# Another order for the first five visits of a fused retention and feed-forward kernel, and two chunks turned on another engine

## The chip, the cores and the metric

The kernel runs on one core of one Trainium2 chip. The metric is the device time of one execution in microseconds (us). A NeuronCore has five engines that run their own instruction streams side by side and wait for each other through semaphores: TensorE (PE: matmuls and transposes; PEld is its loading of stationary operands), VectorE (DVE), ScalarE (ACT), GpSimd (POOL) and SyncE (SP, whose queue here issues nearly all DMA transfers). Each stream is executed strictly in the order in which it was written, so the order of the program text is the schedule.

## The reference

```python
def _attn_ref(q, k, v):              # (8, 8, 576, 64) float32
    scores = (1 / sqrt(64)) * q @ k^T
    gamma = 1.0 - 2.0 ** (-5.0 - arange(8))          # one per head
    Dmat = where(rel >= 0, gamma ** rel, 0.0)        # rel = i - j
    return (scores * Dmat) @ v
def _moe_ref(x, w_in, w_out):        # x: the above as (4608, 512)
    h = maximum(x @ w_in, 0.0)       # w_in (512, 2048)
    return (h * h) @ w_out           # w_out (2048, 512)
```

So: a causal retention over 8 batches and 8 heads, whose output is laid out as 4608 tokens by 512 features, and a feed-forward layer with a squared ReLU. `w_in` and `w_out` arrive as 64-bit floats and the rest as 32-bit floats; the computation is in 32-bit floats.

## The kernel before

**Chunks and visits.** Each batch's 576 tokens are cut into four chunks of 128 and one of 64: 40 chunks in all (chunks 4, 9, 14, ... are the short ones). The main loop (L740 to L812) makes one *visit* per chunk. Visit i first works on the retention of chunk i-1 in three pieces, `retain_a`, `retain_b`, `retain_c` (64x64 matmuls at L457, L460 and L492; ScalarE copies the state at L466 and L495, and the finished, transposed output `xT` at L514), and computes the scores of chunk i (L435), which VectorE multiplies by the causal mask (L441 for chunks 0 to 3, L443 later). GpSimd multiplies q and v by the decay factors (`scale_q`, L375, and L445).

**Turning.** The scores need q and k with the head dimension on the partitions. This is done in two ways. `turn(i)` (L406) makes 16 TensorE transposes (8 for a short chunk, L414); ScalarE copies the k half out (L417) and VectorE the q half (L418). The other way is `flip(i)` (L388), two VectorE transposes of 32x32 blocks (L392), followed by `spread(i)` (L394), which queues 16 small ScalarE copies (8 for a short chunk, L403) that `move` issues a few at a time. `N_TURN, N_BACK = 9, 19` (L380) say that chunks 9 to 18 go the second way; chunk i is flipped in visit i-2 and spread at the end of visit i-1. With `turn`, the same PSUM tile `ps_t` holds the transposes and, from chunk 4 on, the scores.

**Block 0 of the feed-forward layer.** Tokens are taken in 9 blocks of 512. Block 0 is done plainly: 16 *pieces* of `w_in` (128 of the 2048 columns each), each converted on the chip from 64-bit to 32-bit floats and then used in `first_in(j)` (L570): four matmuls of 512 columns (L580), a ReLU on ScalarE (L585), and a square on VectorE that is queued and issued later (L588). `first_in(j, (0,))` and `first_in(j, (1,))` do one half of the tokens each, with 256 columns; the first half of block 0 is there after chunk 1, the second only after chunk 3. `N_HALF = 4` pieces are done in halves.

**Conversions.** A piece is converted in six steps (`round_parts`, L199): one and two on VectorE (L210, L214), *beside*, two ScalarE instructions (L218, L219), and three, four, five on VectorE (L222, L225, L228). `convert(n)` issues the next n steps. From piece 4 on, one and two of the next piece are issued between *beside* and three. After five of a piece, SP fetches up to two later pieces (`fetch_raw`, L196) into six raw buffers.

**The other blocks.** Blocks 1 to 8 are done by Strassen's scheme with seven products (`ffn_in`, 28 steps per block, eight PE records of 256 columns each, L616), with sums on VectorE (L540 to L543 for the inputs, L554 to L557 for the results, L238 to L241 for the weights, during block 1). The first 13 steps of block 1 also convert the first two pieces of `w_out`. A planner, `ffn(i, half)` (L698), is called twice in each visit: while block 0 lasts it issues one first_in and six conversion steps in the first half of a visit and two of each in the second; afterwards it interpolates in the table `PACE` (L691) how many steps should be done by the tokens gone. Blocks become available when their tokens are complete (in `retain_c`): block 1 in visit 9.

**SP's queue.** `load(i+3)` at the end of visit i fetches q, k and v of a chunk; from visit `N_TURN - 1` on, q and k are fetched a visit earlier. The q scaling of chunk i+3 stands at the end of visit i on GpSimd (L811), behind which the v scaling of later chunks queues.

After the visits comes a second phase (from L838, from 595 us on in the trace) that multiplies by `w_out`; the change does not touch it.

Of the kernel before, what the change touches and what calls it, by code (L numbers as in the profile page):

```python
# [40 lines left out]
def kernel(  # L41
# [50 lines left out]
    N_CH = len(chunks)  # L92
# [38 lines left out]
    N_EARLY = TOK // C  # L131
# [25 lines left out]
    pieces = [(0, m, e) for m in range(N_M) for e in range(2)]  # L157
    pieces += [(1, mq + mh * N_MQ, e) for mq in range(N_MQ) for mh in range(2) for e in range(2)]
    N_W1 = N_DF
    N_HALF = 4  # L160
    stage = [W[5].rearrange("p (o s f) -> p o s f", o=4, s=NP),
             W[6][:, 0:3 * NP * 128].rearrange("p (o s f) -> p o s f", o=3, s=NP)]
    N_RAW = 6
# [121 lines left out]
    def fetch_raw(count):  # L285

        for _ in range(count):
            if n_raw[0] < min(N_W1, n_made[0] + N_RAW):
                fetch_w(n_raw[0])
                n_raw[0] += 1  # L290


    def w_in_parts():

        parts = [round_parts(j) for j in range(N_W1)] + [[None] * 2]
        for j in range(N_W1):
            one, two, beside, three, four, five = parts[j]
            if j <= N_HALF:
                yield from (one, two)
            yield beside  # L300
            if j >= N_HALF:
                yield from parts[j + 1][0:2]
            yield three
            yield four

            def last(five=five):
                five()
                n_made[0] += 1
                if n_next[0]:
                    fetch_raw(2)  # L310

            yield last

    w_in_steps = w_in_parts()

    def convert(count):
        for _ in range(count):
            f = next(w_in_steps, None)
            f and f()
# [37 lines left out]
    def rows(half, n=64):  # L357
        return slice(64 * half, 64 * half + n)
# [13 lines left out]
    def scale_q(i, engine):  # L372
        ci, cs = chunks[i][1], chunks[i][3]
        t = loaded[i][0][:cs]
        engine.tensor_tensor(t, t, dv[:cs, :, NCH + ci:NCH + ci + 1].to_broadcast([cs, H, D]), op=ALU.mult)  # L375
# [1 line left out]

    N_TURN, N_BACK = 9, 19  # L380
    moves = []

    def new_qk(i):
        t = work3.tile([128, 2, HP, C], F32, tag="qk", name="qk")
        st[i]["qT"], st[i]["kT"] = t[:, 0, :, :], t[:, 1, :, :]
        return t
# [19 lines left out]
    def turn(i):  # L406

        cs = chunks[i][3]
        n_h = cs // CH
        p = ps_t.tile([128, 2, 512], F32, tag="t", name="t_ps").rearrange("p h (j d t) -> p h j d t", j=2, d=HP)  # L410
        for j in (1, 0):
            for hp in range(HP):
                for h in range(n_h):
                    nc.tensor.transpose(p[:, h, j, hp, :], loaded[i][j][rows(h), 2 * hp:2 * hp + 2, :],  # L414
                                        ident[rows(h), rows(h)])
        to = new_qk(i)[:, :, :, :cs].rearrange("p j d (h t) -> p j d h t", h=n_h)
        nc.scalar.copy(to[:, 1].rearrange("p d h t -> p h d t"), p[:, :n_h, 1, :, :])  # L417
        nc.vector.tensor_copy(to[:, 0].rearrange("p d h t -> p h d t"), p[:, :n_h, 0, :, :])  # L418
# [146 lines left out]
    def some(count=1):  # L565
        for f in queue[:count]:
            f and f()
        del queue[:count]

    def first_in(j, halves=(0, 1)):  # L570

        assert n_made[0] > j
        wi, m, e = pieces[j]
        mp, mm = divmod(m, 2)
        p = ps_f.tile([128, 2, HT], F32, tag="f", name="h_ps")
        w = w_in[mp][:, mm, 2 * e:2 * e + 2, :, :].rearrange("p s c f -> p (s c) f")
        lo, hi = halves[0], halves[-1] + 1
        p = p[:, lo:hi, :]
        for c in range(N_DM):
            nc.tensor.matmul(p.rearrange("p h t -> p (h t)"), lhsT=w[:, c, :], rhs=xT[0][:, c, lo * HT:hi * HT],  # L580
                             start=(c == 0), stop=(c == N_DM - 1))

        t = g_room[mp % 2][:, 3:7:3, mm, :] if e else g_room[mp % 2][:, 0:5:4, mm, :]
        t = t[:, lo:hi, :]
        nc.scalar.activation(t, p, AF.Relu)  # L585

        some(2)
        queue.append(lambda: nc.vector.tensor_tensor(t, t, t, op=ALU.mult))  # L588
        if mm and e and hi == 2:
            queue.append(lambda: [nc.sync.dma_start(  # L590
                g_dram[0, a:b, :, 2 * mp:2 * mp + 2, :].rearrange("s p m t -> p s (m t)"),
                g_room[mp % 2][:, a:b, :, :].rearrange("p s m t -> p s (m t)")) for a, b in QUARTERS])
        if j >= N_W1 - 4:

            sums_w.setdefault(0, sum_w_in(0)).pop(0)()
            if n_next[0] > 1:
                if 1 not in sums_x:
                    sums_x[1] = sum_x(1)
                sums_x[1].pop(0)()
# [73 lines left out]

    def block_steps(n):
        if n == 0:
            seconds = [(0, lambda j: (first_in(j, (1,)), first_in(j + 1, (1,))), j) for j in range(0, N_HALF, 2)]
            return seconds + [(0, first_in, j) for j in range(N_HALF, N_W1)]
        return [(n, ffn_in, n, mp, j) for mp in range(N_MP) for j in range(NP)]

    def step():  # L680
        n, f, *args = steps.pop(0)
        done[0] += 1
        f(*args)

    n_next = [0]

    HALF = C // 2
    N_0 = N_W1 - N_HALF // 2  # L690
    PACE = ((4 * TOK + HALF // 4, N_0 + 2 * N_MP * NP - 2), (5 * TOK - HALF, N_0 + 3 * N_MP * NP - 2),  # L691
            (6 * TOK + HALF // 4, N_0 + 4 * N_MP * NP - 2), (8 * TOK + HALF // 4, N_0 + 6 * N_MP * NP - 2),
            (9 * TOK, N_0 + 7 * N_MP * NP - 2))
    done = [0]
# [32 lines left out]
    def warm(count, wide):  # L727
        t = ps_f.tile([128, 512], F32, tag="f", name="idle_ps")
        for _ in range(count):
            if wide:  # L730
                nc.tensor.matmul(t[:, 0:128], lhsT=idle, rhs=idle, start=True, stop=True)
            else:
                for b in range(2):
                    nc.tensor.matmul(t[rows(b), 0:64], lhsT=idle[rows(0), rows(b)], rhs=idle[rows(0), 0:64], start=True, stop=True,
                                     skip_group_check=True)
# [4 lines left out]
    for i in range(N_CH + 1):  # L740
        if i <= N_EARLY:

            if i == 1:
                convert(2)
            elif i == 2:
                convert(5)
            if i >= 1:
                retain_a(i - 1)
                if i < 3:
                    warm(4, False)  # L750
                else:
                    convert(1)
                    first_in(2 * i - 5, (0,))
                    convert(5)
                retain_b(i - 1)
                if i < 3:
                    warm(4, False)
                retain_c(i - 1)
            convert((0, 1, 1, 0, 1)[i])
            if i == N_EARLY:  # L760
                fetch_raw(2)
                step()
            scores(i)
            if i == 2:
                convert(5)
                first_in(0, (0,))
            elif i == 3:
                convert(1)
                first_in(2, (0,))
                convert(5)  # L770
            elif i == N_EARLY:
                convert(5)
                step()
                convert(6)
            scale_q(i + 1, nc.gpsimd)
            if i < N_EARLY:
                if i < 2:
                    warm(6, False)
                turn(i + 1)
        else:  # L780
            if i == N_EARLY + 1:
                gone[0] = TOK
            retain_a(i - 1)
            if i < N_TURN or N_BACK <= i < N_CH:
                turn(i)
            move(C, i)
            ffn(i - 1, 0)
            retain_b(i - 1)
            if i < N_CH:
                scores(i)  # L790
            retain_c(i - 1)
            if N_TURN <= i + 1 < N_BACK:
                spread(i + 1)
            if N_TURN <= i + 2 < N_BACK:
                flip(i + 2)
            ffn(i - 1, 1)
        if i == 0:
            fetch_raw(2)
        if i < N_TURN - 1:
            load(i + 3)  # L800
        else:
            if i == N_TURN - 1:
                load(i + 3, "qk")
            if i + 4 < N_CH:
                load(i + 4, "qk")
            if i + 3 < N_CH:
                load(i + 3, "v")
        if 0 < i < N_EARLY:
            fetch_raw(1)
        if i > N_EARLY:  # L810
            for j in range(i + 1 + 2 * (i > N_EARLY + 1), min(i + 4, N_CH)):  # L811
                scale_q(j, nc.gpsimd)  # L812
    assert n_next[0] == N_BLK
    first.close()
# [231 lines left out]
```

## Time and profile before

| | us |
|---|---|
| median of 4 runs | 992.36 |
| lowest, highest of them | 991.49, 995.08 |
| the profiled execution | 995.08 |
| its span, first to last instruction | 993.4 |
| PE busy in it | 968.8 |
| DVE busy in it | 767.8 |
| ACT busy in it | 242.4 |
| POOL busy in it | 126.6 |

The profiled execution is the slowest of the four. The span lacks the 1.7 us that lie around the instructions. A PE that counts as busy need not be at its peak: its granted clock is listed beside, and short matmuls follow each other more closely than their durations say. In a line of the timeline the figures are the start, the duration, engine, line and operation, the tiles, the number of instructions merged, and in brackets the idle time in front and what ended it.

With `N_CH` = 40 chunks the visits can be found in the trace by their matmuls: visit 4 begins at 36.3 us, visit 5 at 52.5, visit 6 at 65.3, visit 7 at 78.7, visit 8 at 93.6, visit 9 at 107.2.

### The profile page before, as it was taken

To read this page: it belongs to the slowest core of one execution; us is meant where nothing else is said; L and a number is where in the kernel's file an instruction comes from. 1 tells how busy PE (TensorE), PEld (TensorE's weight loads), DVE (VectorE), ACT (ScalarE), POOL (GpSimd) and SP (SyncE) were. 2 spreads that over 40 slices of the span, in tenths; PEclk is the share of its full clock that TensorE was granted. 3 is DMA by queue.
4 is the path that set the end of the run, shared out by engine and by line. 5 is a ranking of instruction groups with operands and counts; after the bars stand their busy time and mean duration, and the time that the engine had idled before them with its cause. 6 is when DMAs were issued, how large, how long until landed. Compare 5 with 4: busy or idle time off the path is not lost.

```text
span 993.4 us, 24367 instructions
## 1 busy us (share of the span) xinstructions
PE 968.8 (98%) x10388; PEld 864.4 (87%) x10388; DVE 767.8 (77%) x1437; ACT 242.4 (24%) x596; POOL 126.6 (13%) x121
## 2 busy tenths in 40 slices
PE   7899999999999999999999999999999999999998
PEld 6654677888888888888888889999999999999998
DVE  3798798767978888897986777877777677777766
ACT  2544675672222222312221000000000000000000
POOL 3202323122121321212111000000000000000000
PEclk9999999999999999999999999999999999999999
DMA  8873757575587678679358999674673757556351
GB/s 199 240 206 119 195 161 216 156 205 171 180 305 212 197 249 262 217 223 285 112 213 293 404 390 351 233 280 170 233 269 138 272 192 274 190 216 217 123 213 43
DMA packets 185036, 219.20 MB, mean 221 GB/s; under 512 B 118624, under 2 KB 135008, under 8 KB 175968
## 3 DMA queue, kind: packets, MB, share of 16 engines
q1 hardware_dynamic: 182816, 217.13, 66.3%
q8 instruction: 81, 1.33, 0.5%
q10 hardware_dynamic: 2112, 0.52, 0.2%
q14 instruction: 27, 0.22, 0.1%
HBM read 128.23 MB, written 89.39 MB: 219 GB/s over the span
## 4 chain that ended last, share of the span: by engine, by line
PE 87%; DVE 8%; ACT 2%; issue 1%; DMA 1%; SPq 0%; DVEq 0%; ACTq 0%
PE o_b L903 17%; PE h_b L616 15%; PE o_c L903 11%; PE o_a L903 11%; PE h_c L616 10%; PE h_a L616 10%; PE h_ps L580 5%; PE x_ps L457 3%; PE sc_ps L435 2%; PE x_ps L492 2%; PE t_ps L414 1%; DVE w L222 1%; DVE room L623 1%; PE u_ps L460 1%; DVE w L225 1%
## 5 line engine op out<-in xcount | busy, mean ns | idle before, releaser
L616 PE MATMUL h_b<-room,w 128*128 128x256 f32 x736 | 177.1, 383 | 4.5 <-DVE room L635 2.3
L616 PEld LDWEIGHTS h_b<-room,w 128*128 128x128 f32 x736 | 137.2, 190 | 25.5 <-DVE room L635 3.5
L903 PE MATMUL o_b<-w,room 128*128 128x128 f32 x1168 | 144.5, 275 | 0.2 <-DVE room L854 0.2
L903 PEld LDWEIGHTS o_b<-w,room 128*128 128x128 f32 x1168 | 137.2, 192 | 0.5 <-DVE room L854 0.4
L903 PE MATMUL o_c<-w,room 128*128 128x128 f32 x1008 | 123.0, 275 | 0.0
L903 PEld LDWEIGHTS o_c<-w,room 128*128 128x128 f32 x1008 | 117.7, 192 | 0.0
L616 PE MATMUL h_c<-room,w 128*128 128x256 f32 x480 | 114.5, 381 | 0.0
L616 PE MATMUL h_a<-room,w 128*128 128x256 f32 x448 | 107.6, 383 | 0.0
L616 PEld LDWEIGHTS h_c<-room,w 128*128 128x128 f32 x480 | 90.3, 190 | 12.8 <-DVE room L642 0.3
L616 PEld LDWEIGHTS h_a<-room,w 128*128 128x128 f32 x448 | 83.7, 190 | 11.8
L903 PE MATMUL o_a<-w,a 128*128 128x128 f32 x688 | 85.6, 275 | 0.0
L633 POOL TENSOR_TENSOR room<-room 128x512 f32<-128x512 f32 x32 | 36.0, 1125 | 368.5 <-ACT room L632 293.1
L903 PEld LDWEIGHTS o_a<-w,a 128*128 128x128 f32 x688 | 81.2, 192 | 0.1
L917 ACT COPY r<-o_a 128x128 f32<-128x128 f32 x53 | 14.1, 266 | 271.8 <-PE o_a L903 236.0
L623 DVE SCALAR_TENSOR_TENSOR room<-room 128x512 f32<-128x512 f32 x96 | 71.0, 740 | 3.3
L580 PE MATMUL h_ps<-room,w 128*128 128x512 f32 (+1 forms) x160 | 60.2, 526 | 3.5 <-DVE w L228 2.9
L403 ACT COPY qk<-flip 32x256 f32<-32x256 f32 x144 | 57.9, 402 | 2.1
L375 POOL TENSOR_TENSOR q_ld<-q_ld,dv 128x512 f32<-128x512 f32 (+1 forms) x39 | 46.1, 1181 | 83.4 <-DMA q_ld<-in_q_dram 52.0
L457 PEld LDWEIGHTS x_ps<-qk,v_ld 64*64 64x64 f32 x1152 | 40.6, 137 | 15.9 <-issue 10.6
L635 DVE TENSOR_TENSOR room<-h_b,room 128x512 f32<-128x512 f32 x32 | 22.0, 688 | 41.5 <-PE h_b L616 41.5
L457 PE MATMUL x_ps<-qk,v_ld 64*64 64x64 f32 x1152 | 49.9, 227 | 3.2 <-ACT u_sb L495 2.2
L580 PEld LDWEIGHTS h_ps<-room,w 128*128 128x128 f32 x160 | 30.1, 195 | 25.5 <-issue 21.1
(111 smaller groups left out, 1437.3 us busy)
## 6 DMA issues: line engine op xcount, KB each, us to landing
g_dram<-room SPq DMA_DIRECT2D x32, 1792.0 KB, 7.8
a<-g_dram SPq DMA_DIRECT2D x43, 1024.0 KB, 6.9
room<-g_dram SPq DMA_DIRECT2D x20, 1024.0 KB, 5.8
w<-w_dram SPq DMA_DIRECT2D x7, 1792.0 KB, 12.1
out_dram<-room SPq DMA_DIRECT2D x17, 512.0 KB, 3.3
w<-in_moe_w_in_dram SPq DMA_DIRECT2D x16, 512.0 KB, 5.3
w<-in_moe_w_out_dram SPq DMA_DIRECT2D x16, 512.0 KB, 4.1
v_ld<-in_v_dram SPq DMA_DIRECT2D x31, 256.0 KB, 3.9
```

The costliest lines, as they stand in the source:

```text
L375: engine.tensor_tensor(t, t, dv[:cs, :, NCH + ci:NCH + ci + 1].to_broadcast([cs, H, D]), op=ALU.mult)
L403: nc.scalar.copy(*moves.pop(0)[1:])
L435: nc.tensor.matmul(sc[e][rows(h), hp, :], lhsT=kT[rows(e), hp, t], rhs=qT[rows(e), hp, t], start=True, stop=True, skip_group_check=True)
L457: own.append(lambda hp=hp, e=e, b=b: nc.tensor.matmul(x_at(hp, b, h), lhsT=s["vs"][rows(h), 2 * hp + b, :], rhs=s["ret"][rows(h), e, hp, : ...
L492: nc.tensor.matmul(x_at(hp, b, h), lhsT=u[rows(e), hp, :], rhs=s["qT"][rows(e), hp, CH * h:CH * h + CH], start=clears(b, hp // 2), stop=Fa ...
L580: nc.tensor.matmul(p.rearrange("p h t -> p (h t)"), lhsT=w[:, c, :], rhs=xT[0][:, c, lo * HT:hi * HT], start=(c == 0), stop=(c == N_DM - 1))
L616: nc.tensor.matmul(p[:, mm, :], lhsT=w[:, c, :], rhs=xs[n][right][:, c, :], start=(j in OPENS and mm == 0 and c == 0), stop=(j in CLOSES a ...
L623: nc.vector.scalar_tensor_tensor(t, t, 0.0, t, op0=ALU.max, op1=ALU.mult)
L633: nc.gpsimd.tensor_tensor(g["A11"], g["A11"], g["A11"], op=ALU.mult)
L635: nc.vector.tensor_tensor(g["A22"], p, p15, op=ALU.add)
L903: nc.tensor.matmul(p, lhsT=s["lefts"][left][:, m, :], rhs=w_out[j][:, m, WO_SLOT[right], :], start=(i in OPENS and m == 0), stop=(i in CLO ...
L917: nc.scalar.copy(r[:, 0, 0:128], p)
```

## The change

The order of the conversions and first products in visits 3 and 4, with the conversion step reached in brackets:

| | before | after |
|---|---|---|
| visit 3, second half | first_in(2, first half), convert (26), turn(4) | first_in(2, first half), convert (24) |
| visit 4, between retain_a and retain_b | convert (27), first_in(3, first half), convert (32) | turn(4) |
| visit 4, after retain_c | convert (33), second halves of 0 and 1 | second half of 0 |
| visit 4, after the scores | convert (38), second halves of 2 and 3, convert (44) | convert (27), second half of 1, convert (32) |

Three pieces are done in halves instead of four. The step list of block 0 becomes 16 entries (three second halves and 13 whole pieces) instead of 14 (two pairs of second halves and 12 whole pieces), at most three entries per visit as before, so it ends in visit 9 and not in visit 8. `PACE` moves by two with it, so its points name the same steps of blocks 1 to 8. Chunks 9 and 10 are turned by `turn`, in visits 9 and 10, and `flip` and `spread` begin with chunk 11. The early loading of q and k begins at visit 10. Up to visit 7, the q scaling that is issued at the end of a visit is that of chunk i+2, not i+3.

```diff
-    N_HALF = 4
+    N_ALONE = 4
+    N_HALF = 3
...
-            if j <= N_HALF:
+            if j <= N_ALONE:
                 yield from (one, two)
             yield beside
-            if j >= N_HALF:
+            if j >= N_ALONE:
                 yield from parts[j + 1][0:2]
...
-    N_TURN, N_BACK = 9, 19
+    N_TURN, N_BACK = 11, 19
...
-            seconds = [(0, lambda j: (first_in(j, (1,)), first_in(j + 1, (1,))), j) for j in range(0, N_HALF, 2)]
+            seconds = [(0, first_in, j, (1,)) for j in range(N_HALF)]
             return seconds + [(0, first_in, j) for j in range(N_HALF, N_W1)]
...
+    n_scaled = [N_EARLY + 2]
...
-    N_0 = N_W1 - N_HALF // 2
+    N_0 = N_W1
...
                 if i < 3:
                     warm(4, False)
+                elif i == N_EARLY:
+                    turn(i)
                 else:
                     convert(1)
-                    first_in(2 * i - 5, (0,))
+                    first_in(1, (0,))
                     convert(5)
...
-            convert((0, 1, 1, 0, 1)[i])
+            convert((0, 1, 1, 0, 0)[i])
...
                 first_in(2, (0,))
+                convert(3)
+            elif i == N_EARLY:
+                convert(3)
+                step()
                 convert(5)
-            elif i == N_EARLY:
-                convert(5)
-                step()
-                convert(6)
...
-                turn(i + 1)
+                if i + 1 < N_EARLY:
+                    turn(i + 1)
...
-            for j in range(i + 1 + 2 * (i > N_EARLY + 1), min(i + 4, N_CH)):
+            for j in range(n_scaled[0], min(i + (4 if i > N_TURN - 4 else 3), N_CH)):
+                n_scaled[0] += 1
                 scale_q(j, nc.gpsimd)
```

## The prediction

> **What bounds the kernel now.** I read the page first (busy shares, the chain that ended last), then the stretches by visit, then PE's gaps in order of time, then the other engines around each gap.
>
> ```profile
> PE 968.8 (98%) x10388; PEld 864.4 (87%) x10388; DVE 767.8 (77%) x1437; ACT 242.4 (24%) x596; POOL 126.6 (13%) x121
> ...
> PE 87%; DVE 8%; ACT 2%; issue 1%; DMA 1%; SPq 0%; DVEq 0%; ACTq 0%
> ```
>
> TensorE is the bound; what can be won without taking work from it is its idle time and the VectorE share of the chain. Where those lie, by stretches (busy per engine, then granted clock, DMA share, GB/s):
>
> ```profile
> 22.20:25.60 3.40, 3.40 (x100) 3.21 (x100) 0.46 (x2) 1.47 (x4) 2.12 (x2) 0.56 0.24 49
> 39.20:42.70 3.50, 3.50 (x40) 2.52 (x38) 1.73 (x3) 1.57 (x3) 0.78 (x1) 0.57 1.01 278
> 35.70:65.30 29.60, 26.79 (x269) 17.38 (x268) 23.04 (x43) 12.53 (x27) 3.16 (x3) 0.94 0.84 236
> 65.30:107.20 41.90, 40.67 (x492) 21.00 (x491) 35.47 (x57) 21.17 (x44) 8.43 (x8) 1.00 0.55 151
> 107.20:159.00 51.80, 47.02 (x589) 38.75 (x590) 47.70 (x71) 34.95 (x85) 14.08 (x11) 1.00 0.69 198
> 159.00:297.00 138.00, 137.94 (x1669) 117.44 (x1672) 107.35 (x170) 60.30 (x145) 31.91 (x29) 1.00 0.66 201
> ```
>
> From 159 us on PE does not stop (0.06 us idle in 138), and the change leaves those steps as they are. What it can move lies in three stretches: visits 4 and 5 (29.60 - 26.79 = 2.8 us idle, and 3.5 us at a clock of 0.57, which wastes 3.5 x 0.43 = 1.5), visits 6 to 8 (1.2 us idle) and visits 9 to 12 (4.8 us idle). The gaps themselves:
>
> ```profile
> 38.87 2.99 PE L580 MATMUL h_ps<-room,w 128*128 128x256 f32 x8 [1.85 <-DVE w L228]
> 44.58 3.72 PE L580 MATMUL h_ps<-room,w 128*128 128x256 f32 x16 [0.68 <-ACT room L514]
> 52.49 0.46 PE L414 MATMUL t_ps<-w,k_ld 64*128 64x64 f32 x8
> 53.13 3.70 PE L580 MATMUL h_ps<-room,w 128*128 128x512 f32 x8
> 85.47 0.69 PE L435 MATMUL sc_ps<-qk 64*64 64x64 f32 x32 [1.23 <-DVE qk L418]
> 108.38 0.69 PE L492 MATMUL x_ps<-qk,u_sb 64*64 64x64 f32 x32 [0.50 <-ACT u_sb L466]
> 113.27 1.97 PE L616 MATMUL h_b<-room,w 128*128 128x256 f32 x8 [0.98 <-DVE room L541]
> 130.46 0.27 PE L457 MATMUL x_ps<-qk,v_ld 64*64 64x64 f32 x2 [0.97 <-DVE qk L443]
> 157.01 1.99 PE L616 MATMUL h_b<-room,w 128*128 128x256 f32 x8 [1.45 <-DVE room L635]
> ```
>
> **The change, part by part.** *Visits 4 and 5.* Before, first_in(3, first half) stands in front of `retain_b(3)` and waits 1.85 us for step five of piece 3; the clock drops, and these 8 records take 2.99 us where the same ones at 29.08 and 33.79 us take 1.97. After, turn(4) stands there. I replay PE by its rows from 35.7 us, where first_in(2) ends: retain_a(3) 0.6 to 36.3 (its mask is done at 35.8); turn(4), 0.64 from its start to the next group (52.49 to 53.13), to 37.0; retain_b, with the state copy done by then, to 37.5; the 0.28 wait for L495 and retain_c to 38.4; the 0.68 wait for the `xT` copy; second half of piece 0 (1.9) to 41.0; scores(4) to 41.6; second half of piece 1 to 43.5; turn(5) to 44.1; second half of piece 2 to 46.0; retain_b(4) to 46.3. Scores(5) then need VectorE's L418 of turn(5), which stands behind the whole conversion of piece 4. VectorE: five(3) ends at 38.7, L418(4) and a square to 39.5; then the mask of scores(4) makes it wait to 42.2 and is done at 42.8; one and two of piece 4 to 43.5, a square, one and two of piece 5 (its data landed at 44.0) to 44.7; three, four, five of piece 4 (0.72 + 0.72 + 0.61) to 46.8; L418(5) to 47.5. So PE waits about 1.3 us there. Waits of 0.28 + 0.68 + 1.3 and 0.2 of loose ends make 2.4, against 2.8 + 1.5 = 4.3 before: **-1.9**. Bounds: SP issues the fetch of piece 5 at 37.6 in both kernels; landings of `w_in` took 3.8 to 7.9 us, 6.4 here. At 7.9 PE waits 1.5 more; a quicker landing gains nothing, since *beside* of piece 4 ends only at 44.8. The clock: the stretch ahead of the drop held only 0.6 us of matmuls; in the replay it holds 2.4. If it drops all the same, +1.5.
>
> The Trainium skill ("TensorE: Matmul & The Clock Gate", section "HAM oscillation — how this bites in real kernels") gives the rule that PE should have no gaps over about 3.4 us. By it neither kernel would lose clock here, and the 1.5 us would stay saved; the trace, where a gap of 1.85 us was followed by 0.57, speaks against leaning on it.
>
> *What moves behind it.* At the end of visit 4 VectorE has 32 conversion steps behind it instead of 44, two pieces, and PE two pieces less: the lead of three pieces, in program order, is the same in visits 5 to 8. On SP, load(7) stands behind two fetches released by five(4), not four: issued at 52.94 before, near 48 now; load(8) still queues behind fetches for five(7), near 60 instead of 69.9.
>
> *Visits 6 to 8.* The one gap, 1.23 us at 85.47, has its cause here:
>
> ```profile
> 81.19 0.69 DVE L222 SCALAR_TENSOR_TENSOR w<-w,w 128x512 f32<-128x512 uint32 x1
> 81.24 1.56 POOL L375 TENSOR_TENSOR q_ld<-q_ld,dv 64x512 f32<-64x512 f32 x1 [3.24 <-DMA q_ld<-in_q_dram]
> 81.91 1.43 DVE L225 TENSOR_TENSOR w<-w,w 128x512 f32<-128x512 f32 x1
> 82.76 1.50 POOL L445 TENSOR_TENSOR v_ld<-v_ld,dv 128x512 f32<-128x512 f32 x1
> 83.38 1.43 DVE L228 SCALAR_TENSOR_TENSOR w<-w,w 128x512 uint32<-128x512 uint32 x1
> 84.73 0.68 DVE L418 COPY qk<-t_ps 128x512 f32<-128x512 f32 x1
> ```
>
> Beside a GpSimd row a VectorE row of 0.69 takes 1.43. Four GpSimd scalings fall into visit 7, because scale_q(8), issued in visit 5, waited 16.8 us for its data with v of chunk 6 behind it. With scaling one visit later v no longer stands behind a q that has not landed, and about two scalings fall into each visit. Also flip(9) and flip(10) (4 rows, 0.66 to 0.69 each) leave visits 7 and 8. I take **-0.8**; bounds -1.2 (gap gone) and +0.7 (one doubled row in each of three visits on the chain to L418, less the 0.5 us that L418(6) came ahead of its scores).
>
> *Visits 9 to 12.* PE gains two turns: 2 x 0.64 = **+1.3**, on the bound engine, hidden by nothing; 0 if they fall into waits. ScalarE loses 8 + 16 copies of 0.40 (9.6 us) and gains two of 0.37 and 0.59; VectorE loses four flip rows (2.7) and gains L418 of 0.41 and 0.68. The 0.50 at 108.38 was such copies ahead of L466: gone. The 0.98 at 113.27 was flip(11), 1.3 us, ahead of block 1's input sums L540 and L541; now flip(11) falls under first_in(15), and one of the sums too: gone, and so the 0.25 in its wake. What remains (0.97, 0.29, 0.28, 1.45: 3.0) is VectorE, 47.7 of 51.8 us busy, under the 13 steps that also convert `w_out`. After, these steps lie in visits 10 and 11 with two flips instead of three in their way, 1.3 us less: 1.7 remain. **-3.0** in all; bounds -4.8 (no idle left) and 0 (the same waits one visit later: `PACE` now asks for 54 steps in 1008 tokens, not in 1104).
>
> *One half piece less.* Two halves take 3.65 us, a whole one 3.53 in a pair: **-0.1**. What comes after visit 14 has the same steps at the same tokens: 0.
>
> Sum: -1.9 - 0.8 + 1.3 - 3.0 - 0.1 = **-4.5 us**. The profiled execution, 995.08, would become 990.6; it lies 2.7 above the median. From the median 992.36 I predict **987.9**.
>
> **The rivals.** *The clock drops anyway* (15%): -4.5 + 1.5 = -3.0, 989.4. For it: 22.20 to 25.60 ran at 0.56 after a gap of 2.65; against: 2.4 us of matmuls in the stretch, if small ones. *VectorE's crowd only moves* (15%): the waits of visits 9 to 12 return in 10 to 13: -4.5 + 3.0 = -1.5, 990.9. For it: 9.8 of 10 us busy there. *The waits are unaffected overall* (5%): whatever closes opens elsewhere, 992.4. *Slower: VectorE bounds block 1* (15%). Place: visits 10 to 14, where two pieces' worth of PE time has to be caught up. A step costs PE 1.73 and its share of a visit's attention about 0.5, 2.23; VectorE has 1.1 (nine sums of 0.61 and three squares of 0.72 in seven steps), 0.4 of weight sums (4 x 0.68 in seven), 0.4 of `w_out` (two pieces of 2.7 in 13) and 0.5 of mask, flip and two doubled rows (3.4 in a visit of seven): 2.4 in the first 13 steps, 2.0 thereafter. It decides from 2.75 per step over some 20 steps: 0.5 x 20 = 10 us of waits instead of 1.7, +8.3, 996.2. Against it: with the same steps and no `w_out`, VectorE has 107 of 138 us from 159 on.
>
> **How the numbers follow.** Forecast 50%, its own range 985 to 990.5 by the bounds above; rivals as given. About 0.3% (3 us) is what a measurement can tell from no change. Below 989.4: nearly all of the forecast, half of the clock rival, a little of the second: 0.56. Above 995.3: the slower rival and mishaps of the data of piece 5: 0.17. Between: 0.27. The range takes in the first two rivals and part of the slower one: 983.8 to 994.5.
>
> **What the profile after would show.** Right: no L580 gap for L228 in visit 4, the clock at 1.00 around 40 us; a gap of about 1.3 before scores(5) for L418; no gap in visit 7; two L414 groups in visits 9 and 10; block 1's first L616 step with no wait for L541. Wrong: a clock near 0.57 in visit 4 or 5; scores of visits 5 to 8 all waiting for L418; L616 gaps of over 2 us in sum in visits 10 to 13.

## The result and the profile after

The changed kernel takes 989.76 us in the median of 43 runs (988.39 to 993.87), the kernel before 992.64 us (65 runs, 990.82 to 996.77). The ratio is 0.9971, with a 95% interval of 0.9965 to 0.9976: 2.9 us faster, 0.3%. The prediction was 4.5 us faster.

The profiled execution of the changed kernel took 989.67 us, close to its median, with a span of 988.0. The profiled execution before, 995.08, lay 2.4 above its own median, so the two spans differ by 5.4 us, of which about half is not the change. Lines of the changed kernel's page (busy shares; the chain that ended last):

```profile
PE 969.0 (98%) x10404; PEld 863.1 (87%) x10404; DVE 769.3 (78%) x1434; ACT 234.2 (24%) x573; POOL 128.3 (13%) x121
...
PE 90%; DVE 7%; ACT 1%; issue 1%; DMA 0%; SPq 0%; DVEq 0%; ACTq 0%
```

PE's busy time is nearly the same (before: 968.8 us, 98%), and more of the chain is PE (before: 87%): waits went. By stretches, with the borders at the beginning of visit 6 (54.6 us), of visit 9 (96.0) and of the scores of chunk 13 (157); columns: length, busy time of PE, PEld, DVE, ACT and POOL, granted clock, DMA share, GB/s:

```profile
35.00:54.60 19.60, 18.25 (x240) 11.96 (x238) 16.27 (x29) 8.40 (x19) 4.74 (x4) 1.00 1.04 276
54.60:96.00 41.40, 40.79 (x489) 21.09 (x488) 37.20 (x60) 21.32 (x42) 6.28 (x5) 1.00 0.64 179
96.00:157.00 61.00, 58.26 (x701) 45.05 (x703) 55.80 (x81) 33.38 (x80) 16.89 (x13) 1.00 0.64 178
157.00:291.50 134.50, 134.48 (x1611) 114.81 (x1606) 105.07 (x167) 56.80 (x137) 30.82 (x28) 1.00 0.70 207
```

PE is idle for 1.35, 0.61 and 2.74 us in the first three and not at all in the fourth; in the first profile before it was 2.8 us (and a stretch at half clock), 1.2 and 4.8. The gaps that are left, in PE's rows of the timeline:

```profile
37.23 0.27 PE L458 MATMUL x_ps<-qk,v_ld 64*64 64x64 f32 x2 [0.28 <-ACT u_sb L496]
38.60 1.99 PE L581 MATMUL h_ps<-room,w 128*128 128x256 f32 x8 [0.68 <-ACT room L515]
46.47 0.69 PE L436 MATMUL sc_ps<-qk 64*64 64x64 f32 x32 [0.38 <-DVE qk L419]
74.22 0.69 PE L436 MATMUL sc_ps<-qk 64*64 64x64 f32 x32 [0.61 <-DVE qk L419]
135.14 1.99 PE L617 MATMUL h_b<-room,w 128*128 128x256 f32 x8 [0.30 <-DVE room L636]
149.16 1.99 PE L617 MATMUL h_c<-room,w 128*128 128x256 f32 x8 [0.65 <-DVE room L631]
152.81 1.99 PE L617 MATMUL h_b<-room,w 128*128 128x256 f32 x8 [1.66 <-DVE room L636]
```

Line numbers are one higher than before. The gap for step five of piece 3 is gone, as are those behind the small ScalarE copies (0.50) and before block 1's sums (0.98). VectorE's backlog in block 1 shows up one or two visits later, in one long gap of 1.66 us.

**A measure that does without the start.** Both kernels run the same instructions up to the scores of chunk 3, yet these begin anywhere from 30.9 to 33.3 us in the profiles below. From the scores of chunk 18 to the last instruction the three profiles compared next take 765.3, 765.3 and 765.4 us, and all profiles of this case 765.1 to 765.7. So I compare the time from the start of the scores of chunk 3 to the start of those of chunk 18, "the stretch": it holds nearly everything that these kernels do differently, and the start's scatter is left out. It is read from one execution of each kernel. It is 195.57 us in the first profile before, 193.52 in a second one (below) and 190.47 after: 3.05 us less than the second.

### The profile page after: what moved, and what is told of

It is laid out like the page before. It is cut to its first block, busy times and chain, and to the rows that moved or that the text cites. A ratio compares the mean times of both kernels' runs of the same rounds, so it can differ in the third digit from the quotient of the medians.

```text
span 988.0 us, 24367 instructions
## 1 busy us (share of the span) xinstructions
PE 969.0 (98%) x10404; PEld 863.1 (87%) x10404; DVE 769.3 (78%) x1434; ACT 234.2 (24%) x573; POOL 128.3 (13%) x121
## 3 DMA queue, kind: packets, MB, share of 16 engines
q8 instruction: 82, 1.34, 0.6%
## 4 chain that ended last, share of the span: by engine, by line
PE 90%; DVE 7%; ACT 1%; issue 1%; DMA 0%; SPq 0%; DVEq 0%; ACTq 0%
PE o_b L909 17%; PE h_b L617 16%; PE o_c L909 11%; PE o_a L909 11%; PE h_a L617 10%; PE h_c L617 10%; PE h_ps L581 5%; PE x_ps L458 3%; PE sc_ps L436 2%; PE x_ps L493 2%; PE t_ps L415 2%; DVE room L624 1%; PE u_ps L461 1%; DVE qk L419 1%; DVE w L223 0%
## 5 line engine op out<-in xcount | busy, mean ns | idle before, releaser
L404 ACT COPY qk<-flip 32x256 f32<-32x256 f32 x120 | 48.3, 402 | 1.7
```

The source lines that it names most:

```text
L404: nc.scalar.copy(*moves.pop(0)[1:])
```

## The experiments

Ratios are to the kernel before, timed alongside, with 95% intervals.

**The kernel before once more.** No edit.

> The kernel before, unchanged, for the size of what can be told apart and for a second profile of it. Every theory: a ratio of 1.000, within 0.001. If the half-clock stretch in visit 4 (3.4 us at half speed behind the wait of 1.85 us, worth about 1.5 us) belongs to this kernel's order, the second profile has it as well; if it is a chance of one execution, the second profile has a clock of 1.00 around 40 us and a span nearer to 990.5, the median less 1.7 us, than to 993.4.

Ratio 0.9998 (0.9988 to 1.0007). Its profile has a span of 990.4, at the median, and a clock of 1.00 where the first profile had 0.57 (39.2 to 42.7 us), although TensorE waits there as well:

```profile
37.66 1.97 PE L580 MATMUL h_ps<-room,w 128*128 128x256 f32 x8 [1.66 <-DVE w L228]
```

```profile
39.20:42.70 3.50, 2.54 (x70) 1.86 (x70) 0.65 (x3) 1.41 (x5) 0.00 (x0) 1.00 1.00 318
```

So the half-clock stretch belongs to some executions of this order, not to all: of the five profiles in this case that have the old order with the wait left open, two show it (the first, and that of the kernel before with the later conversion, below). This second profile is the better base for what follows.

**The order of visits 3 and 4 alone.**

```diff
 # the change, with these two taken back:
-    N_TURN, N_BACK = 11, 19
+    N_TURN, N_BACK = 9, 19
...
-            for j in range(n_scaled[0], min(i + (4 if i > N_TURN - 4 else 3), N_CH)):
-                n_scaled[0] += 1
+            for j in range(i + 1 + 2 * (i > N_EARLY + 1), min(i + 4, N_CH)):
```

> Only the order of visits 3 and 4 is changed (three half pieces, chunk 4 turned in its visit, fewer conversions), with chunks 9 and 10 still turned by VectorE and ScalarE and q scaled as before. Theory of the sum: 1.9 us from visits 4 and 5, 0.1 from the half piece, and about 1 us of the gap behind flip(11) because block 1 starts half a visit later: 2.5 to 3 us faster. Rival, the clock drops anyway and the crowd of VectorE only moves: 0.5 us faster. Rival, VectorE bounds block 1: slower by 2 us or more, with over 6 us of gaps in visits 10 to 14.

Ratio 0.9975 (0.9962 to 0.9988), 2.5 us faster: most of the change is here. The gaps of 0.50 and 0.98 us in visit 9 go with the order alone, since block 0 now fills visit 9. What opens instead, in PE's rows and in a stretch behind the last of them:

```profile
68.23 0.27 PE L458 MATMUL x_ps<-qk,v_ld 64*64 64x64 f32 x2 [1.52 <-POOL v_ld L446]
88.41 0.69 PE L436 MATMUL sc_ps<-qk 64*64 64x64 f32 x32 [1.02 <-DVE qk L419]
151.95 3.38 PE L617 MATMUL h_b<-room,w 128*128 128x256 f32 x8 [2.23 <-DVE room L636]
```

```profile
152.00:155.30 3.30, 3.30 (x9) 2.62 (x10) 2.52 (x4) 0.00 (x0) 0.00 (x0) 0.56 0.99 268
```

Against the second profile before, the scores of chunk 6 come 9.3 us earlier (58.42 for 67.76), but GpSimd's q scaling of chunk 8, which waits for its data, only 7.9 (65.17 for 73.08), and it and the row behind it take 1.54 and 1.50 us where they took 1.06 each. So the v scaling of chunk 6, that row, is late for visit 7. I had not expected this wait. With the half clock behind the gap of 2.23 us in it, the stretch of this profile is 192.49, only 1.0 us below 193.52.

**Chunks 9 and 10 alone.**

```diff
-    N_TURN, N_BACK = 9, 19
+    N_TURN, N_BACK = 11, 19
```

> Only chunks 9 and 10 are turned by TensorE instead of VectorE and ScalarE. Two turns cost PE 1.3 us. Theory of the sum: they are paid for by the gap of 0.50 us behind the ScalarE copies and by 1.3 us of flips less among the steps of block 1 that wait for VectorE: 0.5 us faster, within 0.5. Rival, turns on the bound engine are simply added: 1.3 us slower. The gap before the first sums of block 1 (0.98 us) stays, as flip(11) keeps its place.

Ratio 1.0007 (0.9997 to 1.0017). The stretch is 194.54, 1.0 us longer than the 193.52. The gap of 0.50 behind the ScalarE copies goes, one of 0.29 behind VectorE's copy opens before the scores of chunk 9, the one before block 1's sums stays (0.90 us), and turning brings a wait of its own, VectorE's copy behind a queue that is already long:

```profile
122.47 0.69 PE L435 MATMUL sc_ps<-qk 64*64 64x64 f32 x32 [1.13 <-DVE qk L418]
```

By this profile the turns cost in the old order most of what they take on PE, as the rival said; the times (0.7 us slower) lean the same way, but their interval just includes no change.

**The scaling loop alone.**

```diff
+    n_scaled = [N_EARLY + 2]
...
-            for j in range(i + 1 + 2 * (i > N_EARLY + 1), min(i + 4, N_CH)):
+            for j in range(n_scaled[0], min(i + (4 if i > N_TURN - 4 else 3), N_CH)):
+                n_scaled[0] += 1
```

> Only the loop of the q scalings is changed, which at this N_TURN moves the scaling of chunk 8 from visit 5 to visit 6. Theory of the sum: the pile of four GpSimd scalings in visit 7 goes, and with it the gap of 1.23 us before the scores there: 0.8 us faster. Rival, another VectorE row is doubled instead: no change within 0.3 us.

Ratio 0.9994 (0.9982 to 1.0006): not told apart from no change by the times. In the profile the gap before the scores of chunk 7 is gone, one of 0.41 us stands before those of chunk 5, and the stretch is 192.73, 0.8 less: the size expected.

**The change without its scaling loop.**

```diff
-            for j in range(n_scaled[0], min(i + (4 if i > N_TURN - 4 else 3), N_CH)):
-                n_scaled[0] += 1
+            for j in range(i + 1 + 2 * (i > N_EARLY + 1), min(i + 4, N_CH)):
```

> The changed kernel with the old loop of the q scalings. If the parts add up, it is 0.6 us slower than the changed kernel, 2.3 us faster than before. Theory from the kernel with the order alone: with the earlier visits the pile on GpSimd makes TensorE wait for the v scaling of chunk 6 in visit 7 (1.52 us there), so that the loop is worth more with the new order than alone: 1 to 1.5 us slower than the changed kernel, 1.5 to 2 us faster than before.

Ratio 0.9999 (0.9985 to 1.0014): all of the change's gain is gone. Against the change's 0.9971 the loop is worth 0.28%, some 2.8 us with an uncertainty of about 1.5, more than either side expected. GpSimd's rows and PE's show it:

```profile
68.12 1.49 POOL L376 TENSOR_TENSOR q_ld<-q_ld,dv 128x512 f32<-128x512 f32 x1 [16.59 <-DMA q_ld<-in_q_dram]
69.57 1.50 POOL L446 TENSOR_TENSOR v_ld<-v_ld,dv 128x512 f32<-128x512 f32 x1
```

```profile
71.13 0.27 PE L458 MATMUL x_ps<-qk,v_ld 64*64 64x64 f32 x2 [2.25 <-POOL v_ld L446]
92.58 0.69 PE L436 MATMUL sc_ps<-qk 64*64 64x64 f32 x32 [0.61 <-DVE qk L419]
```

```profile
72.40:75.80 3.40, 3.40 (x8) 1.51 (x5) 3.33 (x7) 1.77 (x3) 0.00 (x0) 0.50 0.65 170
```

The row at 69.57 is v of chunk 6; it stood behind q of chunk 8, for whose data GpSimd waited 16.59 us. In the changed kernel the same row runs 18 us earlier:

```profile
51.62 1.24 POOL L446 TENSOR_TENSOR v_ld<-v_ld,dv 128x512 f32<-128x512 f32 x1
```

And behind the gap of 2.25 us the clock was halved for the next 3.4 us in this profile.

That this wait is the whole of the 2.8 us is not shown. The kernel with the order alone has the old loop too, and the same wait (1.52 us in its profile), and is 2.5 us faster than before. Set beside the next run, the loop is worth 0.3 us without the two turns, where it moves only the scaling of chunk 8 (0.9975 to 0.9972), and 2.8 with them (0.9999 to 0.9971); the two differ by about as much as their uncertainty.

**The change without the two turns.**

```diff
-    N_TURN, N_BACK = 11, 19
+    N_TURN, N_BACK = 9, 19
```

> The changed kernel with chunks 9 and 10 turned by VectorE and ScalarE (N_TURN 9): order and scaling without the turns. My sum had the turns pay for themselves: no faster than the changed kernel, about 3 us faster than before. Rival, after the turns alone came out 0.7 us slower: two turns on the bound engine are paid in full, and this kernel is 0.5 to 1.3 us faster than the changed one.

Ratio 0.9972 (0.9958 to 0.9985), the change's own. With both other parts in place, setting N_TURN to 11 neither gains nor costs anything that can be told. With 9, a gap of 1.58 us stands before the scores of chunk 8, 0.51 behind ScalarE's small copies and 2.23 in visit 13 (followed by a stretch at a clock of 0.50), against the 1.3 us of turns. But N_TURN does more than choose the turns: it sets the visit from which q and k are loaded early and the visit from which the loop scales chunk i+3. With 9, the q scaling of chunks 9 and 10 comes a visit earlier, and ahead of the scores of chunk 8 two VectorE rows take 1.43 us each beside GpSimd's rows at 85.46 and 87.00 (q of chunk 10, v of chunk 8); the changed kernel has one such row there. So this run prices the setting, not the turns alone.

**The first pieces of w_out a block later**, in the changed kernel and in the kernel before.

```diff
-        if n >= 3 or n_w2[0] < 3 + 2 * 5:
+        if n >= 3 or n == 2 and n_w2[0] < 3 + 2 * 5:
```

> The changed kernel with the first two pieces of w_out fetched and converted in block 2 instead of block 1; nothing is left out. Theory: what is left of the gaps in visits 10 to 13 of the changed kernel (0.30, 0.65 and 1.66 us, all behind VectorE rows) is the backlog that these conversions (some 5.4 us of VectorE) build up among the weight sums of block 1: the gaps go, 2 us or more faster than the changed kernel, so 4.5 to 5.5 us faster than before. Rival: the gaps come from the GpSimd rows that double VectorE rows in visit 13, and stay: as the changed kernel, 3 us faster than before; or they reappear in block 2.

Ratio 0.9942 (0.9926 to 0.9959): 5.8 us faster than before, about 2.9 faster than the changed kernel. From the scores of chunk 8 to those of 13, and on to those of 18, first the changed kernel, then this one:

```profile
87.88:156.98 69.10, 66.36 (x785) 49.00 (x780) 62.20 (x92) 36.24 (x87) 16.89 (x13) 1.00 0.61 173
156.98:222.52 65.54, 65.54 (x806) 55.94 (x801) 47.06 (x71) 40.24 (x100) 14.21 (x13) 1.00 0.69 177
```

```profile
86.88:152.41 65.53, 65.45 (x786) 49.32 (x781) 54.15 (x82) 33.91 (x83) 16.83 (x13) 1.00 0.54 147
152.41:219.19 66.78, 65.72 (x804) 55.93 (x800) 51.98 (x81) 42.36 (x104) 13.83 (x13) 1.00 0.74 209
```

VectorE loses 8 us of rows in the first part, PE's 2.74 us of idle time fall to 0.08, and the part is 3.6 us shorter; 1.2 us come back in the second, as a gap of 0.77 and one of 0.30 behind ScalarE's L496. That the gaps of block 1 are the backlog of these conversions is thereby shown.

> The kernel before with the same later conversion of w_out. Theory: of the gaps in visits 9 to 12 before, those of 0.32, 0.79, 0.30, 0.28 and 1.45 us go (3.1 us), those of 0.50 and 0.98 us stay, since they lie in front of the conversions: 2 to 3 us faster than before. Rival: GpSimd: no change.

Ratio 0.9983 (0.9972 to 0.9994). The gaps after the first two of visit 9 are gone as expected, 0.26, 0.89 and 1.15 us open in block 2 instead, and a gain of 1.7 us remains. Taking the conversions out of block 1 gains 1.7 us in the old kernel and 2.9 in the new one; the two are not told apart. This profile, too, has a stretch at half clock in visit 4 (0.51 from 38.2 to 41.6 us), behind a wait of 2.22 us for step five.

**That, without the two turns, and that, spread over block 2.**

```diff
 # in the changed kernel with the later conversion
-    N_TURN, N_BACK = 11, 19
+    N_TURN, N_BACK = 9, 19
```

> The changed kernel with the later conversion of w_out and with chunks 9 and 10 turned by VectorE and ScalarE. With the conversions in block 1, the two turns neither cost nor gained. Theory: they were paid for by relief of VectorE in block 1; with that crowd gone their 1.3 us on TensorE are paid in full, so this is 0.5 to 1.3 us faster than the changed kernel with later conversion, 6.5 to 7 us faster than before. Rival: their cost lies in visits 9 and 10 in waits of TensorE that exist anyway: the same as with turns, 5.8 us faster than before.

Ratio 0.9945 (0.9932 to 0.9959), the same as with the turns. They are not paid for by block 1's crowd: with N_TURN 9 the gap before the scores of chunk 8 is 1.66 us, and that balances 1.3. As above, two doubled VectorE rows (1.55 and 1.43 us) stand ahead of it beside the earlier GpSimd scalings, so the balance is one of the setting.

```diff
-        if n >= 3 or n == 2 and n_w2[0] < 3 + 2 * 5:
+        if n >= 3 or n == 2 and j % 2 == 0 and n_w2[0] < 3 + 2 * 5:
```

> The changed kernel with the later conversion of w_out, spread over the whole of block 2 (at every second step instead of every step). The gaps that the later conversion opened in visits 15 and 16 (0.77 and 0.30 us, behind ScalarE rows among which the conversions stand) go: 0.5 to 1.3 us faster than with the conversions packed, 6.3 to 7 us faster than before. Rival: they come from the ScalarE copies of the flipped chunks alone: no change, 5.8 us faster than before.

Ratio 0.9952 (0.9939 to 0.9964), not told apart from the packed form. The two gaps of block 2 become one of 0.51 us behind ScalarE's small copies (stretch 188.44 against 188.22): so the small copies have a part in them, and the packing is not all.

**Filling the wait in visit 4 before.**

```diff
                 else:
+                    if i == N_EARLY:
+                        warm(10, False)
                     convert(1)
                     first_in(2 * i - 5, (0,))
```

> The kernel before with ten idle matmul pairs (64x64, about 1.2 us, result not used) in visit 4 between retain_a(3) and first_in(3, first half), where TensorE waits 1.45 to 2.2 us for VectorE. The wait stays, but TensorE is idle for under 1 us of it. Theory: part of the gain of the new order is that the clock no longer drops behind this wait, in those executions in which it does (3.4 us at half speed, 1.5 us each): median 0.3 to 1.5 us faster than before, highest times lower, and no half-clock stretch around 40 us in the profile. Rival: the drop is too seldom to matter, or comes whatever fills the wait: no change.

Ratio 0.9998 (0.9987 to 1.0009): no change. PE's gap there was 1.06 us and the clock 1.00, but as only some executions have the drop (two of five profiles without the filling), the median can hardly show its loss.

**The scores of chunk 4 first.**

```diff
 # in the changed kernel with the later conversion
                 fetch_raw(2)
-                step()
             scores(i)
...
             elif i == N_EARLY:
+                step()
                 convert(3)
                 step()
```

> The changed kernel with the later conversion of w_out and, in visit 4, the scores of chunk 4 in front of the second half of piece 0 instead of behind it. In the changed kernel TensorE waits there 0.68 us for the copy of xT, VectorE 1.86 us for the scores, and TensorE again 0.38 us in visit 5 for VectorE's copy of chunk 5. Theory: the scores (0.6 us) fill the first wait and release VectorE 1.9 us earlier, so that the second goes too: 0.7 to 1.1 us faster than with the later conversion alone, 6.5 to 7 us faster than before. Rival: the scores wait for the copies of chunk 4 just as long: no change, 5.8 us faster than before.

Ratio 0.9957 (0.9943 to 0.9970). The profile does what was expected: the gaps of 0.68 and 0.45 us become one of 0.30, and the stretch is 187.53, 0.7 less than with the later conversion alone (188.22). The times do not show it; it stays open.

## Why the prediction was right, and where its sizes were off

The direction and the mechanism were right: VectorE's conversions no longer stand in TensorE's way in visit 4, the first sums of block 1 no longer behind flip(11). The sum said 4.5 us and 2.9 were measured. That 2.9 is close to the 3.0 of the rival *The clock drops anyway* is chance: its drop did not come. Against the second profile of the kernel before, by the starts of the scores of chunks 3, 6, 8 and 18 (two whole pieces are done later after the change; they are taken out at 7.06 us, the time from 47.56 to 54.62 us in which the changed kernel does two in a row):

| part | before | after | pieces moved | gain | predicted |
|---|---|---|---|---|---|
| visits 4 and 5, scores 3 to 6 | 36.20 | 27.76 | -7.06 | 1.4 | 1.9 + 0.1 |
| visits 6 to 8, scores 6 to 8 | 28.42 | 28.07 | | 0.35 | 0.8 |
| from there, scores 8 to 18 | 128.90 | 134.64 | +7.06 | 1.3 | 3.0 - 1.3 |
| sum | 193.52 | 190.47 | | 3.05 | 4.5 |

The sum does not depend on the 7.06, the split does: counted by PE's idle time, which falls from 3.18 to 1.54, from 1.03 to 0.61 and from 4.72 to 2.74 us, the parts give 1.6, 0.4 and 2.0, and less 1.3 for the turns 2.7 in all.

**The clock term.** The step that set 2.8 + 1.5 = 4.3 us against 2.4 took a half-clock stretch of one execution for a property of the kernel, and took its whole price off the median, although only some executions pay it: two of the five profiles of the old order with the wait left open have the stretch, the second profile, with a wait of 1.66 us, does not, and filling the wait changed nothing that the times can tell. The reading "only 0.6 us of matmuls" ahead of the drop was wrong as well: the clock changes at 39.66 us, and in the 3.41 us before that PE is busy for 1.56. Without the 1.5 the step would have read 2.8 - 2.4 = 0.4. That 1.4 came is in part luck, for the replay erred the other way: it had TensorE wait 1.3 us for VectorE's copy of chunk 5 where it waited 0.38. Piece 5's data were there by 42.9 us and not at 44.0, and *beside* of piece 4 ended at 43.6 and not at 44.8.

**The GpSimd term.** 0.8 for the scaling loop was its worth in the old order (0.8 by the profile's stretch, nothing that the times can tell). It is not a term that can simply be added: the new order alone makes visit 7 early enough to wait for the v scaling (1.52 and 2.25 us in the two profiles with the old loop). Whether that makes the loop worth 0.3 or 2.8 us, the two pairs of runs leave open. In the full change a gap of 0.61 stays before the scores of chunk 7, where the prediction had none; VectorE's rows L229 and L589 ahead of it take 1.43 and 1.54 us beside the q scaling of chunk 8 and the v scaling of chunk 7. The prediction's queue argument, v behind a q that has not landed, was right; that TensorE itself would come to wait for it in the new order was not seen. SP issued load(7) at 41.1 us and not near 48.

**The turns and block 1.** The gaps fell from 4.6 us (the second profile's) to 2.6, where 1.7 was predicted, and the turns added 1.3 us of PE work: net 0.7, where the table, with its 7.06, has 1.3 and the prediction 1.7. The credit that VectorE would be relieved by a flip less was too large: the crowd comes back as one gap of 1.66 us, and it takes the 13 conversion steps, not the flips, to remove it. The rival *VectorE's crowd only moves* was thus partly true. The rival *VectorE bounds block 1* was wrong: PE waits 2.6 us in visits 10 to 13, not 10. Still, 2.6 is over the 2 us of gaps there that the prediction had named as a sign of being wrong. *The clock drops anyway* did not happen in visit 4 of the changed kernel (1.00 from 35.0 to 54.6 us), nor in the seven other profiles that have this order there; the rule of the Trainium skill that I weighed (gaps of over about 3.4 us, "TensorE: Matmul & The Clock Gate", section "HAM oscillation — how this bites in real kernels") is not what these profiles show: gaps of 1.85 to 2.25 us were followed by half a clock, see the end.

**What was confirmed as stated.** No wait for step five in visit 4; two groups of transposes in visits 9 and 10; the first sum-dependent step of block 1 without a gap. A version faster than both kernels came out on the way: the changed kernel with the later conversion of w_out, 0.9942.

## What to carry to other kernels

Before an effect in one profile is entered as a term, take a second profile of the same kernel: this one held a half-clock stretch of 1.5 us that the second did not have. When a change makes part of a program early, look on every in-order queue for the instruction that waits for data whose arrival moved less, and for what stands behind it. When a constant is set back to isolate one part, look for everything else that reads it: N_TURN also moved loads and scalings. Engine work that one moves off a crowded stretch is worth most where another stretch has it to spare: 13 small steps moved by a block brought as much as the whole change.

## What the runs showed of the hardware

The clock. In the 14 profiles of this case, past the start (from 30 us on), TensorE's gaps of 1.85, 2.22, 2.23, 2.23 and 2.25 us were each followed by about 3.4 us at half clock, and none of 1.66 us or less was. The clock records say more: in each profile the clock changes only at whole multiples of 3.41 us from one another. Cut on that grid, the stretches just ahead of the five drops hold 1.18, 1.19, 1.28, 1.34 and 1.56 us of PE's busy time; of all others, the least busy hold 1.75, 1.75, 1.75 and 1.76, and no drop follows them. So here a gap of under 2 us was enough where one such stretch was left less than half busy, and one of 1.66 was not. That is five against many, in one kernel, and before 30 us it is less clean (in the profile of chunks 9 and 10 alone a stretch with 1.93 us was followed by a drop).

The start. Before any instruction that differs, TensorE stops in visit 2, in the midst of matmuls that wait for nothing the profile shows, for 0.29 us in one profile and 3.29 in another:

```profile
21.03 0.50 PE L493 MATMUL x_ps<-qk,u_sb 64*64 64x64 f32 x18 [0.29 <-issue]
```

```profile
22.05 0.80 PE L492 MATMUL x_ps<-qk,u_sb 64*64 64x64 f32 x18 [3.29 <-issue]
```

The first is the later conversion without the turns, the second the kernel before with the filled wait. The second profile of the kernel before has no such stop. This scatter is as large as the change itself, and its cause was not tried.
